# Moving four things in a fused attention and maxout kernel: copies of queries, masks, one load, and tile placement

## The chip, the core and the metric

The kernel runs on one core of a Trainium2 chip. The core has a matrix engine (TensorE, PE in the profile, with its weight loads listed apart as PEld), three elementwise engines (VectorE or DVE, ScalarE or ACT, GpSimd or POOL), and SyncE (SP), which here only issues DMAs. Each engine takes its instructions from its own queue in program order; between engines they wait on semaphores. The metric is device time in microseconds (us).

## The reference

Two stages with a change of layout between them. The weights come as 64-bit floats, everything else as 32-bit floats.

```python
# q, k, v: (8 batches, 8 heads, 576 rows, 64)
scores = matmul(q, k.T) / sqrt(64)
gamma  = 1 - 2.0 ** (-5 - arange(8))                 # one per head
Dmat   = where(i >= j, gamma[h] ** (i - j), 0)       # causal decay
attn   = matmul(scores * Dmat, v)
x      = attn.transpose(0, 2, 1, 3).reshape(4608, 512)
h      = maximum(maximum(x @ w1, x @ w2), x @ w3)    # w1, w2, w3: (512, 768)
out    = h @ w_out                                   # w_out: (768, 512)
```

## The kernel before

**Tiles and blocks.** The 4,608 rows are 9 tiles of 512 tokens (`NT`), and a tile is 4 blocks of 128 rows (`C`, `CPT`), so there are 36 blocks. While the feed-forward part of tile t runs, the attention of the four blocks of tile t + 1 is woven into it: `steps(t + 1)` holds twelve slots, `ffn(t)` yields between them. For tiles from the third on, each pair of blocks a, b gets: transposes of b, then scores of a and b two slots later, then values of a and b and the transposes of the next block. Work of VectorE, ScalarE and GpSimd that belongs to attention is not issued at once but put in a list, `urgent`, by `soon` (from tile 1 on); the feed-forward part takes one from it after every second of its own products or so, and `scores` and `values` empty it first. So the order on each engine is what the program writes, and a wait of one instruction holds all behind it on that engine.

**Attention of a block from the fifth on (`chunk_scores`, L285).** Attention is done in chunks of 64 rows with a running state. A block has two chunks, c = 0 and 1, and holds all eight heads side by side (a tile of 64 x 512). First TensorE makes two things in two PSUM tiles `sk`: the new part of the state, key times value, `sk<-va,kraw` (L292), and the scores, key times query, `sk<-m,kT` (L296). Then VectorE multiplies the scores by the causal mask and the key decay, `m<-sk,gm` (L300, `mask`), and adds the new state part to the old, `va<-sk,va` (L308, `keep_chunk`; at the start of a sequence ScalarE copies it instead, L306); after chunk 1 GpSimd multiplies the state by its decay, `va<-va,gs_of` (L310). `values` (L351) multiplies masked scores by values and queries by the state in one matmul each, `o<-m,va` (L375), and VectorE applies the query decay and writes the tile's input, `xT<-o,gq`.

**The tiles m.** For that one matmul, a tile `m` has in one half of its partitions the queries of a chunk, and in the other half the masked scores. So `m0` and `m1` of a block hold chunk 0's and chunk 1's queries, and masks go where queries are not. For blocks from the seventh on (`BY_PE`; blocks are counted from 0) VectorE transposes keys and queries, both chunks in one instruction each (L252): the queries of both chunks land in `m1`, those of chunk 0 in `m1[half(1)]`, where chunk 1's masked scores go later. L254 therefore copies them to `m0` on ScalarE. (The profile shows these transposes and copies under L175 or L182, the line from which the list is emptied.) For earlier blocks TensorE transposes and ScalarE copies (L264).

**Feed-forward.** Tile 0 and a third of tile 1 compute the three products plainly (L668), while VectorE and ScalarE turn 64-bit weight words into 32-bit floats (`convert_all`; its bits are loaded by `load_weights`, L422). From then on `up` (L616) replaces a group of 24 products of 128 x 128 by 128 x 256 with 20, made from sums of inputs and of weights (a scheme in the manner of Strassen's). `PRODUCTS` (L66) lists them in order with the PSUM chain each one belongs to:

```python
PRODUCTS = """E a11 b12, E a14 b42, B s15 n5, A a22 b21, C s3 b23, B s19 b41, A s10 b32, C a13 b31, B s6 n2, A s13 b22,
              C a11 b11, B s14 n1, A s11 n4, D s7 b43, B a23 n6, A s20 b33, D s16 b13, B a21 n3, A a21 n8, A a24 n7"""
```

A chain such as B has one PSUM tile, `b`, to which its products add one after another (L645). Between two of them the sum so far is needed by itself, so ScalarE copies it out, `part<-b` (L630), and VectorE combines such copies (`JOINS`, L625). Because the next product writes the same PSUM tile, TensorE's next B waits for ScalarE's copy of the last. Twenty such products for each of six blocks of the hidden dimension make a tile; then the output product, with seven products in the same manner (`downs`, L464).

**Loads and storage.** All loads but three small ones go through SyncE's queue, in program order; at the start (L746 on) these are queries, keys and values of the first blocks and the first weights. `const.tile` places tiles one behind the other in each partition of SBUF; `FILL` (L54, L129) pads that pool by 224 bytes.

## Time and profile before

| | |
|---|---|
| median of 3 runs | 838.05 us (835.22 to 841.33) |
| the profiled execution's own time | 833.2 us |
| its span, first to last instruction | 831.5 us |
| mean granted TensorE clock | 0.973 |
| busy: TensorE, VectorE, ScalarE, GpSimd | 770.2, 597.9, 352.1, 121.8 us |
| copies of queries on ScalarE (26 under L175, 3 under L182) | 614 and 615 ns each |

The page and the views come from one execution. A row of a group gives line, engine, operation and tiles, its count, busy time, the mean of one in ns, and the idle time just before, with what ended it. A row of the waits gives who waited for whom: sum in us, count, longest. A row of the timeline gives start in us, duration, instruction, and in brackets the idle time of the engine before it and what ended that. The granted clock is TensorE's, as a share of full speed. An idle engine matters only where another, in the end TensorE, waits for it.

### The profile page before, as it was taken

The page shows a single profiled execution, that of the slowest core. Times are in us where ns is not written, and L with a number is a line of the kernel's source. Part 1 is how long each engine was busy: PE and PEld are TensorE (multiplying, and loading weights), DVE is VectorE, ACT ScalarE, POOL GpSimd, SP SyncE. Part 2 cuts the span into 40 slices and gives each one's busy share as a digit, 9 for nine tenths or more (in the row PEclk, how much of TensorE's full clock was granted, in tenths as well). Part 3 has the DMA queues.
Part 4 walks back from the last instruction along what each step waited for, and adds up shares of the span by engine and source line. Part 5 has one row for each costly group of instructions (what it writes and reads, how often), then busy time and mean ns, then how long its engine had stood idle before and what let it go on. Part 6 is the DMA issues. An engine that isn't in the chain of part 4 may idle for free. (4 is left out here: it accounts for less than half of the span.)

```text
span 831.5 us, 16050 instructions
## 1 busy us (share of the span) xinstructions
PE 770.2 (93%) x6040; PEld 615.9 (74%) x6040; DVE 597.9 (72%) x1270; ACT 352.1 (42%) x869; POOL 121.8 (15%) x138
## 2 busy tenths in 40 slices
PE   8699989989997999889978999799978997899998
PEld 6444434678886888778867888688867886788887
DVE  2899998888786767667784849676767577484762
ACT  2675641253354425441534334442534153423661
POOL 2310112202120201102020203010211102010100
PEclk9999999999999999999998999999999999899999
DMA  9999832432242215230424124221514041001001
GB/s 198 207 194 181 214 54 71 83 64 40 69 85 52 52 57 93 41 67 26 92 42 68 43 61 81 51 52 59 95 30 75 26 92 38 0 15 39 1 0 51
DMA packets 230109, 59.39 MB, mean 71 GB/s; under 512 B 210960, under 2 KB 228752, under 8 KB 230032
## 3 DMA queue, kind: packets, MB, share of 16 engines
q1 hardware_dynamic: 229456, 58.04, 35.3%
q8 instruction: 47, 0.77, 0.4%
q10 hardware_dynamic: 576, 0.33, 0.2%
q14 instruction: 30, 0.25, 0.1%
HBM read 48.89 MB, written 9.44 MB: 70 GB/s over the span
## 5 line engine op out<-in xcount | busy, mean ns | idle before, releaser
L625 DVE TENSOR_TENSOR part<-part 128x256 f32<-128x256 f32 x460 | 211.5, 467 | 118.5 <-ACT part L630 110.3
L630 ACT COPY part<-b 128x256 f32<-128x256 f32 x230 | 85.6, 372 | 119.3 <-PE b L645 113.4
L630 ACT COPY part<-a 128x256 f32<-128x256 f32 x276 | 102.9, 373 | 76.6 <-PE a L645 67.2
L645 PE MATMUL b<-s,n 128*128 128x256 f32 x276 | 87.5, 400 | 17.1 <-ACT part L630 17.1
L668 PE MATMUL up<-xT,w 128*128 128x512 f32 (+2 forms) x200 | 86.7, 588 | 0.8 <-ACT osb L659 0.8
L645 PE MATMUL a<-s,w 128*128 128x256 f32 x276 | 86.6, 397 | 0.0
L310 POOL TENSOR_TENSOR va<-va,gs_of 64x512 f32<-64x512 f32 x28 | 30.7, 1097 | 329.6 <-DVE va L308 194.3
L645 PEld LDWEIGHTS b<-s,n 128*128 128x128 f32 x276 | 54.5, 201 | 30.1 <-ACT part L630 22.3
L668 PEld LDWEIGHTS up<-xT,w 128*128 128x128 f32 x200 | 37.3, 193 | 44.2 <-issue 39.0
L645 PE MATMUL c<-xT,w 128*128 128x256 f32 x184 | 61.3, 417 | 2.8 <-ACT part L630 2.8
L645 PEld LDWEIGHTS a<-s,w 128*128 128x128 f32 x276 | 54.6, 198 | 8.2
L645 PE MATMUL d<-s,w 128*128 128x256 f32 x184 | 55.5, 383 | 4.3 <-DVE part L625 4.3
L645 PE MATMUL b<-xT,n 128*128 128x256 f32 x184 | 55.6, 384 | 1.2 <-ACT part L630 1.2
L645 PE MATMUL b<-s,w 128*128 128x256 f32 x92 | 30.1, 411 | 19.6 <-ACT part L630 19.6
L462 POOL TENSOR_TENSOR H<-h,H 128x256 f32<-128x256 f32 x24 | 18.4, 768 | 197.5 <-DVE H L461 174.3
L645 PE MATMUL e<-xT,w 128*128 128x256 f32 x184 | 47.2, 379 | 0.0
L645 PE MATMUL a<-xT,n 128*128 128x256 f32 x184 | 47.2, 379 | 0.0
L300 DVE TENSOR_TENSOR m<-sk,gm 64x512 f32<-64x512 f32 x64 | 44.0, 687 | 2.1 <-PE sk L296 0.6
L485 PE MATMUL dx<-To,H 128*128 128x256 f32 (+1 forms) x204 | 44.9, 370 | 0.0
L625 DVE TENSOR_TENSOR h<-part 128x256 f32<-128x256 f32 x92 | 39.1, 425 | 6.9
L645 PEld LDWEIGHTS c<-xT,w 128*128 128x128 f32 x184 | 36.8, 206 | 9.6 <-ACT part L630 3.5
L645 PEld LDWEIGHTS d<-s,w 128*128 128x128 f32 x184 | 35.3, 194 | 10.8 <-DVE part L625 5.9
(120 smaller groups left out, 1362.7 us busy)
## 6 DMA issues: line engine op xcount, KB each, us to landing
bits<-in_moe_w_dram SPq DMA_DIRECT2D x36, 256.0 KB, 6.3
out_dram<-osb SPq DMA_DIRECT2D x35, 256.0 KB, 2.2
kraw<-in_k_dram SPq DMA_DIRECT2D x32, 256.0 KB, 3.7
va<-in_v_dram SPq DMA_DIRECT2D x64, 128.0 KB, 3.7
qraw<-in_q_dram SPq DMA_DIRECT2D x232, 32.0 KB, 2.1
kxraw<-in_k_dram SPq DMA_DIRECT2D x232, 32.0 KB, 2.1
bits<-in_moe_w_out_dram SPq DMA_DIRECT2D x6, 512.0 KB, 6.0
qraw<-in_q_dram SPq DMA_DIRECT2D x6, 256.0 KB, 5.5
```

Of the source, the lines that this page charges most:

```text
L300: nc.vector.tensor_tensor(ms[g, c][half(c)], sk[1 - c][half(c)], gm[half(c)], op=ALU.mult)
L310: nc.gpsimd.tensor_tensor(to[half(1)], to[half(1)], gs_of[half(1)].unsqueeze(2).to_broadcast([D, H, D]), op=ALU.mult)
L462: urgent.append(lambda: (pool(s3, a11, a21, op=ALU.subtract), pool(s4, a12, s2, op=ALU.subtract)))
L485: nc.tensor.matmul(o, lhsT=hS[n](fp)[:, m * P:(m + 1) * P], rhs=late["T"][n][:, fp, cols], start=first and fp == 0 and (m == 0 or last and ...
L625: nc.vector.tensor_tensor(out, a, b, op=op)
L630: nc.scalar.copy(t[:], ps[step[0]][:])
L645: nc.tensor.matmul(ps[chain][:], lhsT=factor(w, fb), rhs=xS[t][x], start=n == 1, stop=ends, skip_group_check=True)
L668: nc.tensor.matmul(ps[:, cols], lhsT=w_sb[i, fb][:, dc * P:(dc + 1) * P], rhs=xT[t][:, dc, cols], start=dc == 0 and cols.start == 0, stop= ...
```

## The change

Four edits.

1. For blocks from the seventh on the copy of chunk 0's queries leaves `transposes`, where it stood behind VectorE's transposes in the list, and stands in `chunk_scores`, issued at once, ahead of the matmuls of scores. These matmuls read chunk 0's queries from `m1`, where the transpose put them, not from the copy in `m0`.
2. In `chunk_scores` the masks of both chunks are put in the list ahead of the two state sums; before, it was sum, mask, sum, mask.
3. The loads of four pieces of weights, issued at the start behind block 4's keys and queries, are issued behind block 4's values.
4. `FILL` is 192 instead of 224 bytes, and `gs_of` (32 bytes) stands directly behind `gk`. Before, `gq` starts at a multiple of 512 bytes and all large tiles behind `gs_of` start 32 bytes past one; after, all start at multiples.

```diff
-FILL = 224
+FILL = 192
...
     gk = const.tile([C, H], FP32, name="gk")
+    gs_of = const.tile([P, H], FP32, name="gs_of")
     one, top, inf, first = (const.tile([P, 1], FP32, name=n) for n in ("one", "top", "inf", "first"))
     const.tile([P, FILL // 4], FP32, name="fill")
     gq = const.tile([P, 2, NP // 2, C], FP32, name="gq")
     gs = raw0.tile([P, NP, D], FP32, name="gs")
-    gs_of = const.tile([P, H], FP32, name="gs_of")
     gm = const.tile([P, H, D], FP32, name="gm")
...
                              raws.pop((n, g))[:].rearrange("a h b i -> a (h b i)")))
-            soon(partial(nc.scalar.copy, m0[half(1)], m1[half(1)]))
             return
...
         sk = [ps_r.tile([P, H, D], FP32, tag="r", name=f"sk{j}") for j in range(2)]
+        of_queries = 0 if g < BY_PE else 1
+        if of_queries:
+            nc.scalar.copy(ms[g, 0][half(1)], ms[g, 1][half(1)])
...
-                nc.tensor.matmul(sk[1 - c][half(c), h, :], lhsT=kT[r, h, :], rhs=ms[g, c][r, h, :],
+                nc.tensor.matmul(sk[1 - c][half(c), h, :], lhsT=kT[r, h, :], rhs=ms[g, c or of_queries][r, h, :],
                                  start=True, stop=True)
...
         for c in range(2):
+            soon(partial(mask, c))
+        for c in range(2):
             if place(g, c) < S // D - 1:
                 soon(partial(keep_chunk, c))
-            soon(partial(mask, c))
...
     load_weights(1)
     load(CPT)
-    load_weights(4)
     decay(0)
...
     load_values(CPT)
+    load_weights(4)
     state(1)
```

The number of instructions on each engine stays; the order on TensorE and GpSimd too. Three queues are reordered. First ScalarE, in tile 7, where block 34's queries (`m_6737`) are transposed. Before:

```order
L630 COPY part<-b 128x256
L630 COPY part<-a 128x256
L175 COPY m_6737<-m_6738 64x512
L630 COPY part<-b 128x256
L630 COPY part<-a 128x256
L630 COPY part<-c 128x256
L630 COPY part<-b 128x256
```

After, the same copy and block 35's stand side by side at the scores of this pair of blocks (L290 is the copy's new line, L633 the copies of sums):

```order
L633 COPY part<-b 128x256
L633 COPY part<-a 128x256
L290 COPY m_6737<-m_6738 64x512
L290 COPY m_6834<-m_6835 64x512
L633 COPY part<-b 128x256
L633 COPY part<-a 128x256
```

The copy stood between copies of sums out of chains a and b while `m1` had just been put on VectorE's list; now the two copies of a pair stand where the pair's scores are computed on TensorE.

Second VectorE, at the scores of blocks 32 and 33, in the same tile (`va` are the states, `part` the joins of the feed-forward). Before, sums (L308) and masks (L300) alternate:

```order
L308 TENSOR_TENSOR va_5955<-sk_6506,va_5953 64x512
L300 TENSOR_TENSOR m_6313<-sk_6507,gm 64x512
L308 TENSOR_TENSOR va_6224<-sk_6507,va_5955 64x512
L300 TENSOR_TENSOR m_6314<-sk_6506,gm 64x512
L308 TENSOR_TENSOR va_6226<-sk_6545,va_6224 64x512
L625 TENSOR_TENSOR part<-part 128x256
L300 TENSOR_TENSOR m_6409<-sk_6546,gm 64x512
L625 TENSOR_TENSOR part<-c,part 128x256
L308 TENSOR_TENSOR va_6404<-sk_6546,va_6226 64x512
L625 TENSOR_TENSOR part<-part 128x256
L300 TENSOR_TENSOR m_6410<-sk_6545,gm 64x512
```

After, each block's two masks (L302) stand ahead of its two sums (L310):

```order
L302 TENSOR_TENSOR m_6313<-sk_6505,gm 64x512
L302 TENSOR_TENSOR m_6314<-sk_6504,gm 64x512
L310 TENSOR_TENSOR va_5945<-sk_6504,va_5943 64x512
L310 TENSOR_TENSOR va_6224<-sk_6505,va_5945 64x512
L302 TENSOR_TENSOR m_6408<-sk_6545,gm 64x512
L628 TENSOR_TENSOR part<-part 128x256
L302 TENSOR_TENSOR m_6409<-sk_6544,gm 64x512
L628 TENSOR_TENSOR part<-c,part 128x256
L310 TENSOR_TENSOR va_6226<-sk_6544,va_6224 64x512
L628 TENSOR_TENSOR part<-part 128x256
L310 TENSOR_TENSOR va_6403<-sk_6545,va_6226 64x512
```

The work is the same; the sum `va_6226` needs `va_6224` after GpSimd has multiplied it by the decay. Before, one instruction stands between the two sums; after, four do.

Third SyncE's queue at the start, from block 4's keys on (`bits` are weight words). Before:

```order
L228 DMA kraw<-in_k_dram 64x8x64 x2
L228 DMA qraw<-in_q_dram 64x8x64 x2
L434 DMA bits<-in_moe_w_dram 64x4x128 x8
L209 DMA va_288<-in_v_dram 64x8x64
L209 DMA va_290<-in_v_dram 64x8x64
L434 DMA bits<-in_moe_w_dram 64x4x128 x4
```

After:

```order
L228 DMA kraw<-in_k_dram 64x8x64 x2
L228 DMA qraw<-in_q_dram 64x8x64 x2
L209 DMA va_276<-in_v_dram 64x8x64
L209 DMA va_278<-in_v_dram 64x8x64
L437 DMA bits<-in_moe_w_dram 64x4x128 x12
```

Block 4's values pass the eight loads of weight words.

## The prediction

> **What bounds the kernel now.** The page first: engine totals and the slices.

> ```profile
> span 831.5 us, 16050 instructions
> PE 770.2 (93%) x6040; PEld 615.9 (74%) x6040; DVE 597.9 (72%) x1270; ACT 352.1 (42%) x869; POOL 121.8 (15%) x138
> ```

> TensorE idles 61.3 us of the span (831.5 − 770.2), the other engines far more, so the question is who holds TensorE. The view of waits, for TensorE and then for ScalarE, answers:

> ```profile
> PE b L645 <- ACT part L630: 37.8, 21, 3.3
> ...
> PE d L645 <- DVE part L625: 4.3, 4, 1.3
> PE c L645 <- ACT part L630: 2.8, 1, 2.8
> ...
> ACT m L175 <- DVE m L175: 41.3, 20, 4.0
> ```

> 40.6 us (37.8 + 2.8, 22 waits) end with one of ScalarE's copies of a sum out of PSUM (L630). ScalarE is 42% busy, so those copies are not slow; something stands ahead of them. The last row names it: ScalarE itself waited 41.3 us ahead of the copy of queries. The timeline of the longest case, ScalarE, VectorE and TensorE in turn:

> ```profile
> 703.71 0.61 ACT L175 COPY m<-m 64x512 f32<-64x512 f32 x1 [3.95 <-DVE m L175]
> 704.35 0.37 ACT L630 COPY part<-b 128x256 f32<-128x256 f32 x1
> ...
> 700.22 0.88 DVE L625 TENSOR_TENSOR part<-part 128x256 f32<-128x256 f32 x2
> ...
> 702.97 0.70 DVE L175 STREAM_TRANSPOSE m<-qraw 128x512 f32<-128x512 f32 x1
> 704.75 0.42 DVE L625 TENSOR_TENSOR part<-e,part 128x256 f32<-128x256 f32 x1 [1.08 <-ACT part L630]
> ...
> 700.05 0.59 PE L645 MATMUL b<-s,n 128*128 128x256 f32 x2
> 700.49 0.59 PE L645 MATMUL a<-xT,w 128*128 128x256 f32 x2
> ...
> 704.77 0.80 PE L645 MATMUL b<-s,w 128*128 128x256 f32 x1 [3.26 <-ACT part L630]
> ```

> Product b was done at 700.64, ScalarE was idle, but its next instruction in order was the copy of queries, whose source VectorE transposed only at 702.97 to 703.67. So b's copy came at 704.35 and TensorE stood for 3.26 us. The same shape recurs in every tile with attention; first and last rows of each size:

> ```profile
> 169.49 0.48 PE L645 MATMUL b<-s,n 128*128 128x256 f32 x1 [0.47 <-ACT part L630]
> ...
> 670.84 0.48 PE L645 MATMUL b<-s,n 128*128 128x256 f32 x1 [0.48 <-ACT part L630]
> ...
> 183.31 0.48 PE L645 MATMUL c<-xT,w 128*128 128x256 f32 x1 [2.75 <-ACT part L630]
> ...
> 258.22 0.48 PE L645 MATMUL b<-s,w 128*128 128x256 f32 x1 [3.26 <-ACT part L630]
> ...
> 270.74 0.48 PE L645 MATMUL b<-s,n 128*128 128x256 f32 x1 [2.12 <-ACT part L630]
> ...
> 720.18 0.48 PE L645 MATMUL b<-s,n 128*128 128x256 f32 x1 [2.32 <-ACT part L630]
> ...
> 239.10 0.48 PE L645 MATMUL b<-xT,n 128*128 128x256 f32 x1 [0.54 <-ACT part L630]
> ...
> 643.71 0.48 PE L645 MATMUL b<-xT,n 128*128 128x256 f32 x1 [0.65 <-ACT part L630]
> ```

> Behind copies of queries lie six waits of 3.26, one of 2.12 and five of 2.32, one of 0.47 and six of 0.48, one of 2.75: 39.4 us. The last two rows (1.2 us) stand behind L306 instead, and 39.4 + 1.2 is the 40.6 of the waits.

> These pauses cost a second time. The windows view over the eight half-clock stretches after the pauses of 3.26 and 2.32 (columns: length, busy time of PE and the others, granted clock; first, last, sum):

> ```profile
> 345.40:348.90 3.50, 3.50 (x10) 2.78 (x9) 0.76 (x2) 1.26 (x4) 0.00 (x0) 0.51 0.44 68
> ...
> 720.90:724.30 3.40, 3.40 (x9) 2.70 (x9) 1.14 (x3) 1.24 (x4) 0.72 (x1) 0.50 0.00 0
> sum 34.30, PE 31.88 PEld 25.54 DVE 9.39 ACT 13.70 POOL 2.23; mean PE 3.98 PEld 3.19 DVE 1.17 ACT 1.71 POOL 0.28
> ```

> TensorE works 31.9 us there at half clock; at full clock that is 15.9 us less.

> **The change part by part.** *Copies of queries.* 29 copies (blocks 7 to 35) of 0.61 us leave the place behind the transposes; the matmuls of scores that read them now read the transposed tile itself. The 39.4 us of idle time and the 15.9 us of half clock are the gain: 55.3. What is late next? VectorE. In the case above its row `part<-e` would run from 703.70, when the transpose ends, to 704.12. The next matmul that needs it is product d, eleven products after b in the list at L66: 0.44 us each (700.49 − 700.05), so at 700.05 + 11 × 0.44 = 704.9. It fits by 0.8 us. For tile 1, with the weight sums on VectorE, the windows say:

> ```profile
> 157.20:220.70 63.50, 60.09 (x502) 51.70 (x501) 55.60 (x126) 23.62 (x64) 12.26 (x13) 1.00 0.27 56
> ...
> 666.70:758.40 91.70, 84.57 (x694) 72.04 (x694) 62.00 (x136) 35.92 (x96) 10.14 (x11) 0.94 0.17 36
> ```

> VectorE is busy 55.6 of 63.5 there, and I give back 1.5 of tile 1's 3.2 us (choice; bounds 0 and 3.2). Tile 7 lasts 91.7 us; less its pauses (0.48 + 3.26 + 2.32) and 0.06 of clock on 84.6 busy us it would be about 81, with 62 of VectorE: room as a whole, though not at every place.

> *The copies' new place* is ScalarE's queue ahead of the scores. Behind them stand the L630 copies, and for those TensorE; and the mask of chunk 1 now waits for the copy. ScalarE around a pair of scores:

> ```profile
> 682.46 0.37 ACT L630 COPY part<-b 128x256 f32<-128x256 f32 x1 [2.74 <-PE b L645]
> ```

> Two copies take 1.23 us of the 2.74 in which it sits idle, while TensorE computes scores. Cost 0. Were the cover gone, 14 pairs × 1.23 = 17 us. At a sequence's start a state copy (L306), which reads the same scores as a mask, now stands behind that mask: in two pairs between the query copies, in others one L630 copy later than before. I choose the 1.2 us that such copies cost today, so no change; bounds 0 and 2.4.

> *Masks ahead of state sums.* VectorE's order changes, not its work:

> ```profile
> 683.82 0.68 DVE L308 TENSOR_TENSOR va<-sk,va 64x512 f32<-64x512 f32 x1 [0.49 <-POOL va L310]
> ...
> 687.82 2.48 DVE L625 TENSOR_TENSOR part<-part 128x256 f32<-128x256 f32 x3
> ...
> 688.05 1.11 POOL L236 TENSOR_TENSOR kraw<-kraw,gk 128x512 f32<-128x512 f32 x1
> ```

> The 0.49 us wait for GpSimd's product goes, since masks now stand between. But that product (L310) then runs beside `part<-part` sums, and such sums suffer: three beside GpSimd took 2.48 us, against 0.88 for two above, so about 0.55 more each. GpSimd's own order is unchanged, its products only come a little later. Gain and loss per pair are about equal; I leave TensorE's 4.3 us of waits for product d as they are, between 0 and 4.3 + 12 pairs × 0.55 = 11.

> [...]

> *Values ahead of weights.* The wait of 4.45 us at the start:

> ```profile
> 39.83 0.34 PE L292 MATMUL sk<-va,kraw 64*64 64x64 f32 x1 [4.45 <-DMA va<-in_v_dram]
> ...
> 37.70 1.51 ACT L264 COPY m<-qt 64x256 f32<-64x256 f32 x4
> ...
> 33.35 0.61 DVE L552 TENSOR_SCALAR expo<-bits 128x512 int32<-128x512 int32 x1 [0.57 <-DMA bits<-in_moe_w_dram]
> ...
> 30.14 1.33 SPq L209 DMA_DIRECT2D va<-in_v_dram  x2
> ...
> 108.63 0.70 PE L655 MATMUL down<-w_out,h 128*128 128x512 f32 x1 [2.20 <-DVE w_out L574]
> ```

> The same scores also need the four query copies that end at 39.21, so only 0.6 us can go. The weights move back by the 1.33 us that SyncE spends on the values, and VectorE already waited for them at 33.35; TensorE needs that weight only after the scores, which covers it. And what is won ahead of 106 us runs into the wait for VectorE's converted output weights at 108.63. I take 0; bounds −4.5 (all of it, should ScalarE's copies come earlier too) and +1.3.

> *Tiles at multiples of 512 bytes.* No row shows a cost of placement. The nearest: `gq` stands at such a multiple already (byte 16,896), `gm` 32 bytes off one.

> ```profile
> L175 DVE TENSOR_TENSOR xT<-o,gq 128x512 f32<-128x512 f32 x28 | 18.5, 682 | 1.6 <-PE o L375 1.5
> ...
> L300 DVE TENSOR_TENSOR m<-sk,gm 64x512 f32<-64x512 f32 x64 | 44.0, 687 | 2.1 <-PE sk L296 0.6
> ```

> 682 against 687 ns: I take 0. Faster DMAs could remove at most the start's waits, within the bounds above.

> Sum, against the profiled execution's own 833.2 us (1.7 of it outside the span): 833.2 − 39.4 − 15.9 + 1.5 = 779.4. The median of the runs is 838.05, 4.85 above the profiled one. If that is more half clock, it goes too; if not, it stays, and the time is 784. I lean to the first and say 781.

> **The rivals.** *VectorE becomes the bound.* In the long case its backlog is 3 us already (`part<-e` could have run from 700.7, and does from 703.7); if more backlog than the 0.8 us of margin gathers, the waits of 3.26 come back as waits of product d: 6 × 3.26 = 19.6, and half clock after some: about 803. For: that margin. Against: it had work for 62 of 91.7 us, and catches up in each group of products. Chance 0.13.

> *The half clock stays.* There are eight stretches for twelve pauses of 2.12 to 3.26 us, so four pauses have none behind them, and another cause is possible: 781 + 15.9 = 797. [...] Chance 0.08.

> *Slower: VectorE's sums lose by the new placement.* Nearly every large tile moves by 32 bytes. If sums of two SBUF tiles grew, VectorE's 62.0 us per tile would bind above 81 (+31%) and make the kernel slower than before above 91.7 (+48%); at +60% a tile takes 99 us, and six of them 6 × 7.5 = 45 us more: about 880. Against: the 682 and 687 ns. Chance 0.03.

> *The change does not do what it says:* something else holds ScalarE at those places, and the time stays near 835. Against: twenty of ScalarE's waits end with that transpose. Chance 0.04.

> **How the numbers follow.** My forecast has 0.72, at 781; with the bounds of the unknown costs 774 to 789. The two nearest rivals reach to 806, and below a full gain at the start and at product d would reach 772; 772 to 806 leaves out the last two rivals and some tails of the others, about 0.17. The three runs differ by 6.1 us, so about 1% (8.4 us) is what a measurement tells from no change. Faster by over 1%: 0.72 + 0.13 + 0.08 = 0.93; within 1% 0.04; slower 0.03.

> **What would show it.** In the waits of after, ScalarE's wait for `m` should be gone and `PE b L645 <- ACT part` fall from 37.8 to under 4; the granted clock from tile 2 on should be 1.00; a tile should take about 81 us. Wrong, if `PE d <- DVE part` exceeds 15 us (VectorE binds), if half clock appears without pauses, or if sums of two SBUF tiles take longer on the mean. Block 4's scores should still start near 39 us, now released by ScalarE.

## The result, and the profile after

The changed kernel takes 781.36 us (median of 4 runs, 780.41 to 782.90), the kernel before in the same comparison 839.69 us (4 runs, 835.22 to 845.43): a ratio of 0.930, 95% interval 0.924 to 0.937. The profiled execution of the changed kernel took 782.9 us. Its page begins:

```profile
span 781.1 us, 16192 instructions
PE 752.1 (96%) x6040; PEld 609.0 (78%) x6040; DVE 614.9 (79%) x1270; ACT 353.4 (45%) x869; POOL 125.0 (16%) x138
```

TensorE idles 29.0 us instead of 61.3, and is busy 18.1 us less for the same 6,040 matmuls. VectorE, though its 1,270 instructions are the same, is busy 17.0 us more. In the view of waits these rows of the changed kernel answer to those quoted before:

```profile
PE d L648 <- DVE part L628: 8.5, 4, 2.3
PE dy L488 <- DVE h L628: 3.8, 3, 2.4
PE sk L298 <- ACT m L263: 2.4, 1, 2.4
PE a L648 <- ACT part L633: 0.7, 3, 0.3
PE b L648 <- ACT part L633: 0.3, 1, 0.3
```

The 40.6 us of waits for ScalarE's copies of sums are 1.0 us now. ScalarE no longer waits for `m`; the group of its copies of queries has hardly any idle time ahead of it (last column):

```profile
L290 ACT COPY m<-m 64x512 f32<-64x512 f32 x29 | 16.7, 613 | 0.4
```

Product d waits for VectorE twice as long as before (8.5 against 4.3 us), and `dy`, an output product that reads `h`, waits 3.8 us instead of 0.5.

To keep the start apart from the rest, the windows view from the end of tile 0's output product to TensorE's last matmul, of the kernel before (columns: length, busy time of PE, PEld, DVE, ACT, POOL, granted clock):

```profile
133.42:828.62 695.20, 649.06 (x5161) 548.67 (x5160) 489.26 (x1075) 280.96 (x750) 97.70 (x107) 0.98 0.26 54
```

and of the changed kernel:

```profile
134.97:778.27 643.30, 629.99 (x5160) 540.47 (x5159) 503.80 (x1075) 281.75 (x748) 101.03 (x107) 1.00 0.28 58
```

This stretch is 51.9 us shorter: 32.8 us less idle time (46.14 to 13.31) and 19.1 us less busy time. The start is 1.55 us longer (133.42 to 134.97). What each edit has in it, the experiments tell.

### The profile page after: what moved, and what is told of

Same layout as the page of the kernel before. It is cut to its first block, busy times and chain, and to the rows that moved or that the text cites. A ratio compares the mean times of both kernels' runs of the same rounds, so it can differ in the third digit from the quotient of the medians.

```text
span 781.1 us, 16192 instructions
## 1 busy us (share of the span) xinstructions
PE 752.1 (96%) x6040; PEld 609.0 (78%) x6040; DVE 614.9 (79%) x1270; ACT 353.4 (45%) x869; POOL 125.0 (16%) x138
## 4 chain that ended last, share of the span: by engine, by line
PE 71%; DVE 16%; DMA 4%; SPq 3%; ACT 3%; issue 2%; POOL 0%; DVEq 0%; ACTq 0%
PE a L648 14%; PE b L648 12%; PE dx L488 10%; PE c L648 6%; DVE part L628 6%; PE dz L488 5%; PE d L648 4%; PE e L648 4%; PE o L378 4%; PE down L658 3%; PE up L671 3%; DVE m L302 3%; PE dy L488 2%; DVE va L310 2%; DMA qraw<-in_q_dram 2%
## 5 line engine op out<-in xcount | busy, mean ns | idle before, releaser
L628 DVE TENSOR_TENSOR part<-part 128x256 f32<-128x256 f32 x460 | 221.8, 492 | 64.1 <-ACT part L633 56.2
L633 ACT COPY part<-a 128x256 f32<-128x256 f32 x276 | 102.7, 372 | 73.5 <-PE a L648 60.5
L633 ACT COPY part<-b 128x256 f32<-128x256 f32 x230 | 85.6, 372 | 101.7 <-PE b L648 93.5
L312 POOL TENSOR_TENSOR va<-va,gs_of 64x512 f32<-64x512 f32 x28 | 33.0, 1178 | 325.8 <-DVE va L310 178.6
L648 PE MATMUL a<-s,w 128*128 128x256 f32 x276 | 82.8, 382 | 0.7 <-ACT part L633 0.7
L648 PE MATMUL b<-s,n 128*128 128x256 f32 x276 | 82.3, 380 | 0.3 <-ACT part L633 0.3
L671 PEld LDWEIGHTS up<-xT,w 128*128 128x128 f32 x200 | 37.6, 194 | 46.2 <-issue 39.4
L648 PEld LDWEIGHTS a<-s,w 128*128 128x128 f32 x276 | 52.0, 190 | 9.0 <-ACT part L633 1.9
L648 PEld LDWEIGHTS b<-s,n 128*128 128x128 f32 x276 | 52.5, 190 | 7.7 <-ACT part L633 0.7
L648 PE MATMUL c<-xT,w 128*128 128x256 f32 x184 | 56.0, 386 | 0.0
L302 DVE TENSOR_TENSOR m<-sk,gm 64x512 f32<-64x512 f32 x64 | 44.0, 687 | 5.1 <-PE sk L298 4.0
L628 DVE TENSOR_TENSOR h<-part 128x256 f32<-128x256 f32 x92 | 42.6, 463 | 6.9
L495 ACT COPY part<-dx 128x256 f32<-128x256 f32 (+1 forms) x34 | 10.5, 362 | 74.1 <-PE dx L488 74.1
L633 ACT COPY part<-d 128x256 f32<-128x256 f32 x92 | 34.2, 372 | 15.3 <-PE d L648 10.1
```

The costliest lines, as they stand in the source:

```text
L302: nc.vector.tensor_tensor(ms[g, c][half(c)], sk[1 - c][half(c)], gm[half(c)], op=ALU.mult)
L312: nc.gpsimd.tensor_tensor(to[half(1)], to[half(1)], gs_of[half(1)].unsqueeze(2).to_broadcast([D, H, D]), op=ALU.mult)
L495: nc.scalar.copy(both[m][:, cols], o)
L628: nc.vector.tensor_tensor(out, a, b, op=op)
L633: nc.scalar.copy(t[:], ps[step[0]][:])
L648: nc.tensor.matmul(ps[chain][:], lhsT=factor(w, fb), rhs=xS[t][x], start=n == 1, stop=ends, skip_group_check=True)
```

## The experiments

Ratios are to the kernel before, timed beside each on the same chip, with 95% intervals.

| kernel | edit | median, us | ratio |
|---|---|---|---|
| `copies_alone` | before + copies of queries moved | 773.70 | 0.924 (0.920 to 0.929) |
| `masks_alone` | before + masks ahead of sums | 845.61 | 1.010 (1.003 to 1.018) |
| `values_alone` | before + values ahead of weights | 837.37 | 0.999 (0.995 to 1.002) |
| `tiles_alone` | before + placement | 834.34 | 0.996 (0.992 to 0.999) |
| `masks_back` | changed kernel, masks as before | 773.25 | 0.924 (0.920 to 0.929) |
| `sums_first` | changed kernel, sums ahead of masks | 765.48 | 0.916 (0.911 to 0.920) |
| `product_on_vector` | changed kernel, GpSimd's product on VectorE | 778.66 | 0.929 (0.926 to 0.933) |
| `on_gpsimd` | before, copies of queries on GpSimd | 775.64 | 0.928 (0.923 to 0.932) |
| `q_first` | before, queries transposed ahead of keys | 799.87 | 0.956 (0.950 to 0.962) |
| `read_only` | before, scores read the transposed tile | 837.34 | 0.999 (0.996 to 1.002) |

### Each edit alone

**Copies of queries.** The kernel before with the first edit:

```diff
-            soon(partial(nc.scalar.copy, m0[half(1)], m1[half(1)]))
...
+            nc.scalar.copy(ms[g, 0][half(1)], ms[g, 1][half(1)])
...
-                ... rhs=ms[g, c][r, h, :],
+                ... rhs=ms[g, c or of_queries][r, h, :],
```

> The kernel before with the first edit alone (copies of queries at the scores, scores read m1). Theory: ScalarE's wait for VectorE's transpose, and the half clock after it, are the whole gain, so this alone gives 778 to 787 us, with ScalarE's waits for m gone. Rival, placement or the order of masks has a part in it: then this stays over 795 us, and one of the other edits alone is clearly faster than the kernel before.

773.70 us: better than predicted for this edit, and better than the whole change. The same stretch of its windows view:

```profile
134.35:768.92 634.57, 627.35 (x5161) 538.80 (x5159) 488.54 (x1075) 282.26 (x748) 98.67 (x107) 1.00 0.29 58
```

Against the kernel before that is 38.9 us less idle time (46.14 to 7.22) and 21.7 us less busy time (649.06 to 627.35). The first was expected; the second is more than the 15.9 us of half clock. The rest is a cost of each pause that I had not seen. TensorE on both sides of a pause in this kernel:

```profile
642.75 0.59 PE L647 MATMUL b<-s,n 128*128 128x256 f32 x2
643.18 0.59 PE L647 MATMUL a<-s,n 128*128 128x256 f32 x2
644.85 0.70 PE L647 MATMUL d<-s,w 128*128 128x256 f32 x2 [1.07 <-DVE part L627]
```

Two matmuls of one product show 0.59 us, but the next pair starts 0.43 us after (642.75 to 643.18): the two overlap by 0.16. Behind the pause of 1.07 us, with no matmul left to overlap with, the pair takes 0.70: 0.27 us of busy time more than 0.43. Twenty pauses are gone, 5.4 us by an estimate from this pair; with the 15.9 that makes 21.3 of the 21.7.

**Masks ahead of sums.**

```diff
         for c in range(2):
+            soon(partial(mask, c))
+        for c in range(2):
             if place(g, c) < S // D - 1:
                 soon(partial(keep_chunk, c))
-            soon(partial(mask, c))
```

> The kernel before with the second edit alone (masks ahead of state sums). Theory: no change, 0.99 to 1.01 of the kernel before, the waits behind copies of queries as before (about 40 us). The joins part<-part grew from 467 to 492 ns on the mean in the changed kernel: if this edit did it, by putting GpSimd's products beside them, they are near 490 here too; if it is only that everything is packed closer, they stay near 467.

The edit makes the kernel before about 1% slower, at the edge of what I expected, and the joins are long here too: 490 ns. From the groups of the kernel before, of the changed kernel, and of `masks_alone` (the last two rows):

```profile
L625 DVE TENSOR_TENSOR part<-part 128x256 f32<-128x256 f32 x460 | 211.5, 467 | 118.5 <-ACT part L630 110.3
L628 DVE TENSOR_TENSOR part<-part 128x256 f32<-128x256 f32 x460 | 221.8, 492 | 64.1 <-ACT part L633 56.2
L626 DVE TENSOR_TENSOR part<-part 128x256 f32<-128x256 f32 x460 | 221.9, 490 | 115.0 <-ACT part L631 107.1
L626 DVE TENSOR_TENSOR h<-part 128x256 f32<-128x256 f32 x92 | 42.7, 464 | 6.9
```

So it is this edit, and not closer packing. The timeline of the changed kernel shows how, VectorE first and GpSimd second:

```profile
641.20 0.68 DVE L302 TENSOR_TENSOR m<-sk,gm 64x512 f32<-64x512 f32 x1
641.81 1.00 DVE L628 TENSOR_TENSOR part<-part 128x256 f32<-128x256 f32 x1
...
645.92 2.79 DVE L628 TENSOR_TENSOR part<-part 128x256 f32<-128x256 f32 x3
```

```profile
646.02 1.23 POOL L312 TENSOR_TENSOR va<-va,gs_of 64x512 f32<-64x512 f32 x1 [3.49 <-PE e L648]
647.33 1.10 POOL L236 TENSOR_TENSOR kraw<-kraw,gk 128x512 f32<-128x512 f32 x1
```

Three joins that would take some 1.3 us take 2.79, beside two GpSimd instructions. All joins together show the same: in the changed kernel 92 of the 552 overlap an instruction of GpSimd and take 812 ns on the mean, and none of the other 460 takes more than 427 ns (from the starts and ends in the trace). The same GpSimd product in the kernel before stood beside a mask, which took its usual 0.69 us:

```profile
687.10 0.69 DVE L300 TENSOR_TENSOR m<-sk,gm 64x512 f32<-64x512 f32 x1
```

```profile
686.74 1.23 POOL L310 TENSOR_TENSOR va<-va,gs_of 64x512 f32<-64x512 f32 x1 [2.95 <-PE b L645]
```

**Values ahead of weights.**

```diff
     load(CPT)
-    load_weights(4)
...
     load_values(CPT)
+    load_weights(4)
```

> The kernel before with the third edit alone (block 4's values ahead of the weights). Theory: the 4.45 us wait for the values goes, but the time is lost again in waits for ScalarE's copies of queries and for VectorE's converted weights, and the plain output product of tile 0 still begins at 106 to 109 us: 0.99 to 1.01 of the kernel before. Rival, the start was bound by that load: 4 us less.

No change, 0.999. The changed kernel, which has this edit, shows where the time goes: block 4's score matmuls now wait for ScalarE's copy of queries (the 2.4 us in its waits) and run at 39.1 us, and tile 0's output product begins at 110.2 us, a little later even than I expected; without the edit, at 108.6 (before) and 109.9 (`copies_alone`). In the profiled execution of `values_alone`, the longest of its ten (846.25 us), the scores run at 42.9 us and that product begins at 115.1, well past the 109 that I expected; over the ten runs there is no change. `tiles_alone`, which lacks this edit, has no wait for the values either (next paragraph: its loads of weight words land in 4.8 us, 6.3 before), so in the changed kernel either edit could have removed it.

**Placement.**

```diff
-FILL = 224
+FILL = 192
...
+    gs_of = const.tile([P, H], FP32, name="gs_of")
```

> The kernel before with the fourth edit alone (tiles at multiples of 512 bytes). Theory: placement costs nothing, 0.99 to 1.01 of the kernel before, mean durations of masks (687 ns), joins (467 ns) and copies (372 ns) within 2%. Rival, placement speeds up VectorE's or ScalarE's instructions or the loads: 8 us or more gone, and a shorter mean of one of these groups or of the time to landing.

Masks (687 ns), joins (468) and copies of sums (373) last as long as before, so no instruction gains. The time is 0.4% lower, clear of no change by little, and I have no cause for it: the stretch behind tile 0 lasts 695.86 us in its profiled execution, 695.20 before, and between `copies_alone` and `masks_back`, which has placement and values on top, there are 0.45 us. But loads land sooner. The DMA issues of the kernel before, and of this one (last column: us from issue to landing):

```profile
bits<-in_moe_w_dram SPq DMA_DIRECT2D x36, 256.0 KB, 6.3
```

```profile
bits<-in_moe_w_dram SPq DMA_DIRECT2D x36, 256.0 KB, 4.8
```

In the six other kernels with the old placement this figure is 5.6 to 6.7, in the four others with the new one 4.6 to 5.0. The start gains nothing by it: TensorE still waits there for VectorE's converted weights (in `tiles_alone` 3.4 us for `w` and 2.2 for `w_out`).

### What about the masks costs time

**Undoing that edit in the changed kernel** (the diff above, reversed):

> The changed kernel with the second edit undone (sum, mask, sum, mask; the other three edits stay). Theory: masks ahead of sums cost 8 us by putting GpSimd's products beside VectorE's joins, so undoing it gives 770 to 776 us, joins part<-part back from 492 to about 470 ns, waits for product d back from 8.5 to about 4.5 us. Rival, the other edits eat what the copies give (copies alone 773.7, all four 781.4): 778 us or more.

773.25 us, 8.1 less than the changed kernel. Its stretch behind tile 0 is 634.52 us, 8.8 less: 6.3 less idle (7.01) and 2.5 less busy time.

```profile
134.73:769.25 634.52, 627.51 (x5160) 538.98 (x5159) 488.25 (x1075) 281.86 (x748) 98.51 (x107) 1.00 0.28 58
```

VectorE works 488.25 us there instead of 503.80. Of 15.6 us that its instructions grew by, TensorE saw 8.8.

**Moving the product to VectorE**, all else as in the changed kernel:

```diff
-                nc.gpsimd.tensor_tensor(to[half(1)], to[half(1)],
+                nc.vector.tensor_tensor(to[half(1)], to[half(1)],
```

> The changed kernel (masks ahead of sums) with the state's product by gs_of made by VectorE instead of GpSimd, 28 instructions of about 0.69 us: 19 us more work for VectorE. Theory: the joins stand still beside these GpSimd products, so they get shorter again (part<-part from 492 to 470 ns or less, h<-part from 463 to 425) although VectorE has more to do; the work saved (14 us) and the work added (19 us) nearly cancel: 775 to 785 us. Rival, the joins are slower because of the order of VectorE's own queue: they stay at 490 ns, and with 19 us more for VectorE the time is 785 us or more.

The joins get short again, 458 ns, while VectorE's queue keeps the new order and has 19.3 us more in it:

```profile
L628 DVE TENSOR_TENSOR part<-part 128x256 f32<-128x256 f32 x460 | 206.4, 458 | 63.2 <-ACT part L633 55.2
L628 DVE TENSOR_TENSOR h<-part 128x256 f32<-128x256 f32 x92 | 39.1, 425 | 6.9
...
L312 DVE TENSOR_TENSOR va<-va,gs_of 64x512 f32<-64x512 f32 x28 | 19.3, 689 | 2.0 <-ACT va L308 1.1
```

The time is even 2.7 us lower than the changed kernel's. So the joins are slow because of GpSimd beside them, not because of the order.

**The opposite order**, both sums and then both masks:

```diff
         for c in range(2):
-            soon(partial(mask, c))
-        for c in range(2):
             if place(g, c) < S // D - 1:
                 soon(partial(keep_chunk, c))
+        for c in range(2):
+            soon(partial(mask, c))
```

> The changed kernel with both state sums ahead of both masks, the opposite of the second edit. GpSimd's product then runs beside the two masks, whose source is in PSUM and which took 687 ns beside it or not. Theory (a join of two SBUF tiles stands still beside a GpSimd instruction, a mask does not): joins part<-part at 470 ns or less, 768 to 776 us, no slower than sum, mask, sum, mask. Rival, any other order than alternation costs time because masks or sums come late: 778 us or more with joins near 470.

765.48 us, below what I expected: the fastest kernel of this study. GpSimd's product is then released one place earlier and falls mostly beside masks: of its 29.1 us, 23.2 lie beside masks and 2.7 beside joins of two SBUF tiles; before the change these are 17.3 and 5.2 us, after it 8.8 and 18.1 (from the starts and ends in the traces). The group of its joins, and its waits for product d (4.3 us before, 8.5 after the change):

```profile
L628 DVE TENSOR_TENSOR part<-part 128x256 f32<-128x256 f32 x460 | 205.3, 456 | 64.6 <-ACT part L633 56.4
```

```profile
PE d L648 <- DVE part L628: 0.5, 2, 0.3
```

In the stretch behind tile 0 TensorE idles 1.2 of 627.72 us:

```profile
134.67:762.39 627.72, 626.55 (x5160) 539.14 (x5159) 481.84 (x1075) 282.23 (x748) 96.71 (x107) 1.00 0.28 59
```

Against `masks_back` that is 6.8 us less: product d's waits are 3.9 us less, and the 1.2 us of waits behind state copies (L308) are gone. How much of it the shorter joins give, and how much the earlier sums and state copies, no run separates.

### What about the copies gives time

**Reading alone**: scores read the transposed tile, the copy stays in its place.

```diff
+        of_queries = 0 if g < BY_PE else 1
...
-                ... rhs=ms[g, c][r, h, :],
+                ... rhs=ms[g, c or of_queries][r, h, :],
```

> The kernel before, only that the scores read chunk 0's queries from the transposed tile and not from the copy; the copy stays where it was on ScalarE. Theory: it is the copy's wait that holds ScalarE, and TensorE behind it, so nothing changes: 0.99 to 1.01 of the kernel before, waits behind copies of queries still about 40 us. Rival, the reading of the copy had a part in it: 8 us or more faster.

0.999, and ScalarE's wait for `m` is the 41.3 us of the kernel before. Reading the transposed tile gives nothing by itself.

**Another engine**: the copy stays in its place and GpSimd makes it.

```diff
-            soon(partial(nc.scalar.copy, m0[half(1)], m1[half(1)]))
+            soon(partial(nc.gpsimd.tensor_copy, m0[half(1)], m1[half(1)]))
```

> The kernel before with the copy of queries left in its place in the program but made by GpSimd instead of ScalarE; scores still read the copy. Theory: the gain came from taking the wait for VectorE's transpose off ScalarE's queue, so TensorE's waits for copies of sums fall from 40 to under 5 us here too; GpSimd's copies (29, of about 1.1 us by its products of that size) stand beside joins and cost some of it: 780 to 800 us. Rival, it was the place of the copy or the tile that scores read: 825 us or more.

775.64 us, with scores that read the copy as before. The wait for the transpose is still there, only in a queue for which nobody waits longer than before (VectorE's waits for GpSimd's product are 5.2 us, 5.5 before):

```profile
POOL m L175 <- DVE m L175: 147.6, 19, 15.7
```

It is faster than I expected. Two terms of that forecast were off: GpSimd copies in 613 ns, not 1.1 us, and the restarts were left out, as in `copies_alone`. The copies do stand beside joins, whose mean is 484 ns here (467 before).

**A smaller dose**: VectorE transposes queries first.

```diff
-            for n, t in (("kx", kT), ("q", m1)):
+            for n, t in (("q", m1), ("kx", kT)):
```

> The kernel before with queries transposed ahead of keys on VectorE, all else as it was; the copy can start earlier by the distance of the two transposes, 1.92 us (701.05 against 702.97) and 0.94 us (717.45 against 718.39). Theory: the waits of 3.26 and 2.32 us become about 1.3 and 1.4, some 20 us less; and as the half clock follows windows with over 2 us of idle, those after such pauses go too, some 16 us more: 795 to 803 us. Rival, the half clock does not depend on the length of the pauses: about 815 us, clock still near 0.97.

799.87 us. TensorE's waits of 3.26 us are 1.34, those of 2.32 are 1.40, and the granted clock of the profiled execution is 0.994 instead of 0.973: no half clock behind tile 0. The row of its waits that was 37.8:

```profile
PE b L645 <- ACT part L630: 19.2, 20, 1.4
```

## Why the prediction came out right

The time was forecast as 781 us and is 781.36. It is right for its main reason, but two of its terms were off, and they cancel: that it comes within 0.4 us is luck.

**Copies of queries: right cause, sized 6.8 us too small.** The theory has four independent runs behind it: the copy moved (773.7), handed to another engine (775.6), held up for less time (799.9), and only read differently (837.3). Of the term, 39.4 us of idle time less the 1.5 us given back made 37.9, and 38.9 came. Tile 1 gave 1.2 us back, a wait of `dy` for VectorE's `h` that `copies_alone` has at 201.65 us; a wait of 0.8 us for ScalarE's `osb`, at 134.23 us before, went as well, which I had not counted. The half clock's 15.9 us came, and with it some 5.4 us (the estimate above) for the twenty restarts, which I left out. Together 60.6 us in the stretch behind tile 0, where I had 53.8.

**Masks ahead of state sums: wrong, taken as 0, cost 8.8 us** (8.1 by the medians). The step that failed is "gain and loss per pair are about equal". The gain, VectorE's waits for GpSimd's product, was 5.5 us at most (`DVE va L308 <- POOL va L310` sums to that before); VectorE's instructions grew by 15.6 us, and ahead of product d, where VectorE is late, TensorE pays for it. Against `masks_back`, product d's waits are 4.1 us longer and those of `dy` 2.5.

I had the row of the slow joins and used its price for the upper bound only, and I misread the price: 2.48 us for three joins against 0.88 for two is 0.39 us more for each, not 0.55, and 0.39 is also what the 92 joins beside GpSimd lose on the mean (812 against 422 ns). One sign of being wrong that I had named came true by this, longer sums of two SBUF tiles (492 ns, 467 before), through GpSimd and not through placement.

What the runs show is this: joins of two SBUF tiles were stretched beside GpSimd (in the changed kernel 812 ns on the mean, 422 without), masks from PSUM were not (686 beside one of its instructions, 688 without; from the starts and ends in the trace), and `product_on_vector` takes those GpSimd instructions away, and the added stretching goes with them (`part<-part` 458 ns on the mean, 492 in the changed kernel). That a join stands still beside a GpSimd instruction, the theory in two of the expectations, was not shown: measured are the longer joins, 0.39 us more on the mean.

**Values: right**, 0 within the interval, and for the reason given: the scores then wait for ScalarE.

**Placement: right as far as instructions go.** Group means are the same; 0.4% in one comparison remains unexplained.

**The distance of profile and median: right.** The 4.85 us by which the median lay above the profiled run go with half clock, as far as the mean clock of each run tells: of 19 runs of the kernel before, those with a mean clock of 0.977 took 832.4 to 835.8 us, those with 0.964 or 0.965 took 839.7 to 844.2. With the pauses this spread is gone too: `copies_alone` ranges from 773.2 to 776.0.

**The sum as measured:** −60.6 (copies) + 8.8 (masks) = −51.8 in the stretch behind tile 0, where the profiles differ by −51.9; the start adds 1.55, of which I know no cause (in `copies_alone`, whose start is as before, it is 0.93 longer). That is 50.3 us from 833.2 to 782.9 in the profiled executions. I had 53.8.

**The rivals.** "VectorE becomes the bound" named the right place, waits of 2.04 to 2.33 us for product d in four tiles, but not the cause: with the copies alone these waits are 1.05 to 1.35 us, near the 0.90 to 1.28 before. That the half clock stays was wrong: behind tile 0 `copies_alone` has none and the changed kernel one window of it, behind the last of those waits. Why some pauses have none behind them, the last section shows. No sum became slower by placement.

## What to carry to other kernels

An instruction that waits in an in-order queue costs what stands behind it (here copies of queries that waited 41.3 us on ScalarE made 39.4 us of TensorE's pauses): look for the engine that is idle and late at once, and put the copy where its source is long done (0.924 of the time before), or in a queue on which nobody waits (0.928). When the order of VectorE's work is changed, look at what GpSimd is released to do by it. In the changed kernel masks, with a PSUM source, took as long beside GpSimd's instructions as without (686 and 688 ns), joins of two SBUF tiles did not (812 and 422): there the first belong beside GpSimd's instructions and the second elsewhere. A pause of TensorE cost more than its length here: 0.27 us for the restart in the case above, and half clock behind eight of the twelve of 2.12 to 3.26 us (next section).

## What the runs showed of the hardware that was not expected

```profile
355.68:359.09 3.41, 1.09 (x5) 0.66 (x5) 2.37 (x6) 1.26 (x3) 0.00 (x0) 1.00 0.07 11
359.09:362.50 3.41, 3.41 (x10) 2.70 (x9) 1.41 (x4) 1.12 (x3) 0.72 (x1) 0.50 0.43 66
536.59:540.00 3.41, 1.81 (x9) 1.25 (x7) 3.20 (x8) 1.15 (x4) 0.00 (x0) 1.00 0.18 36
540.00:543.41 3.41, 2.69 (x12) 2.39 (x13) 1.62 (x4) 2.26 (x7) 0.72 (x1) 1.00 0.37 57
```

The first pause lies in one window, which has 2.32 us without a matmul, and the next window is at half clock. The second lies across two windows, with 1.60 us in the first, and nothing happens. I did this for the twelve profiled executions between 70 and 755 us, for windows at full clock with 1.4 us or more of idle time: behind all 53 with at least 2.02 us came half clock, behind none of the 33 with at most 1.95 us; of the four between, behind two. So the limit is near 2.0 of 3.413 us here. That is why twelve pauses had eight stretches behind them. It would also explain why equal runs of the kernel before differ by up to 1.4%, if the raster falls elsewhere in each: `read_only`, with twelve pauses of the same lengths, has ten such stretches. For the runs without a trace this is not shown.

**GpSimd's copy of 64 x 512 took 613 ns**, ScalarE's 614: a copy is not to be priced from GpSimd's products of that size (1,097 ns).
